# Stage 1 of a fused attention and MoE kernel: three loads issued earlier on SP, one later load pinned in the queue

## The chip, the cores and the metric

One core of a Trainium2 chip runs the whole program. The time is device microseconds of one execution. The profile is one execution of its own, with its own time; times of other runs are given as medians.

## What is computed

Three stages run in one program, all in float32: multi-head attention with rotary embedding, a gated MLP with a spatial mix over the sequence, and a causal attention with four experts of which two are taken.

```python
# batch 4, heads 8, seq 576, head_dim 64
q_rot, k_rot = rotate(q), rotate(k)
scores = scale * q_rot @ k_rot.T ; attn = softmax(scores) ; x = attn @ v      # stage 1
h = gelu(x @ w_in) ; u, v = split(h) ; x = x + (u * (w_sg @ norm(v) + b)) @ w_out   # stage 2
out = top-2-of-4 experts of causal attention over x                           # stage 3
```

The change touches stage 1 alone: the attention, and the conversion of w_in that runs beside it for stage 2. That weight comes as 64-bit words and is turned into a pair of float32 parts (high and low) by ACT, DVE and POOL.

## The kernel before, in words

Stage 1 works on pairs of heads: 4 batches of 4 pairs, 16 pairs, called pair 0 to pair 15 here (the third pair is pair 2). A pair takes nine slots, 0 to 8, one for each 128 rows of scores of one head (slot 8 holds the last 64 rows of both). The loop at the end of the stage runs `slot(k)` for k from 0 on, with pair n = k // 9 and slot x = k % 9, and after it one step of the w_in conversion in the slots that `W_AT` names: slot 7 of pair 0; slots 3 to 6 of pair 1; slots 2 to 4 of even pairs; slots 0 to 3 of odd ones.

The products of a pair need its query copies and its key copies in a layout for TensorE. For pair n+1 they are made inside pair n. `load` brings q and k with their rotary partners (`t0` is q, `t1` is k, 576 KB each) into tiles that have two buffers each, so a load for pair n+2 must wait until pair n's rotated q or k has been read for the last time. `rope` rotates them on POOL: two products and a sum for each (for pair n+2: q in slot 4 and k in slot 7 of pair n, and in slots 7 and 8 for pair 2). `parts` then splits them: DVE (ACT for pair 1) casts to the high part `hi`, POOL subtracts to get `lo`, and SP issues DMAs that copy both into place: `fill_q`, six copies, in slot 1 of the pair before, and `fill_k`, four copies into `kh`, in slot 3 of the pair before. The first product that needs them is the one for slot 0 of the new pair, issued in slot 8.

The order of the work on PE, ACT, DVE and POOL is the program's order, written by hand. The SP queue is different. A planner orders the DMAs that are not pinned by when it expects their inputs and buffers, so it may issue a load long before its place in the program. `tc.keep_in_program_order` pins a DMA directly behind the DMA that precedes it in the program text on the same queue. Pinned before the change are: the inputs of pairs 0 and 1, all values (`load_values`, 320 KB, three buffers), and the words of w_in (`load` in `convert_in`, 512 KB, two buffers). All DMAs of this stage go through SP, and SP issues them one after another; one that waits holds up all behind it.

The lines that the steps below use: L361 to L376 (inputs and values), L154 (key copies), L169 (query copies), L511 (results out), L174 (row factors out), L598 (w_in). Operations of the four engines carry the line of a helper, L59, and are told apart by their tiles.

Of the kernel before, what the change touches and what calls it, by code (L numbers as in the profile page):

```python
# [15 lines left out]
B, H, S, D = 4, 8, 576, 64  # L16
# [3 lines left out]
NP = H // 2  # L20
# [6 lines left out]
def f(ap):  # L27

    return ap.bitcast(F32)
# [15 lines left out]
def fused_kernel(ctx, tc, qk, v, w_in, w_out, w_sg, g_ln, b_sg, wqk, wvg, wo, rope, cst, out):  # L45
    nc = tc.nc
# [26 lines left out]
    def bank(t):  # L73
        shape = [P, 2, 512] if t.isupper() else [P, 512]
        return ps[t].tile(shape, F32, tag="b", name="ps_" + t)
# [22 lines left out]
    def split(hi, lo, src, engine=POOL):  # L98
        ACT.copy(hi, src)
        engine.tensor_tensor(lo, src, f(hi), op=ALU.subtract)  # L100
# [81 lines left out]
    def ahead(load, n):  # L182

        t = load(0)
        for c in range(n):
            u, t = t, load(c + 1) if c + 1 < n else None
            yield u
# [136 lines left out]
    with ExitStack() as st:  # L324
# [30 lines left out]
        class Work:  # L355
# [3 lines left out]
            def load(self, n):  # L359
                self.n, self.b, self.p, self.pr = n, n // NP, n % NP, prs[n % 2]  # L360
                self.ts = []  # L361
                for x in range(2):
                    self.ts.append(ld.tile([P, 2, S], F32, tag=f"t{x}", name=f"t{x}"))
                for x in (1, 0) if n < 2 else (0, 1):
                    d = nc.sync.dma_start(self.ts[x], qk[self.b, self.p, :, x])
                    if n < 2:
                        tc.keep_in_program_order(d)
                    if n == 0 and x == 1:
                        for i in range(2):
                            tc.keep_in_program_order(nc.sync.dma_start(rp[:, i], rope[:, i]))  # L370
                if n == 0:
                    tc.keep_in_program_order(nc.sync.dma_start(ident, cst[:, 0:P]))

            def load_values(self):
                self.vt = ld.tile([P, NKB, 2, D], F32, tag="v", name="v", bufs=3)
                tc.keep_in_program_order(nc.sync.dma_start(self.vt, v[self.b, self.p]))  # L376

            def first(self):

# [146 lines left out]
        def slot(k):  # L526


            n, x = divmod(k, 9)
            (nk, xk), (nn, xn) = divmod(k - 1, 9), divmod(k + 1, 9)  # L530
            w, p, wk, wn, nx = [works.get(i) for i in (n, n - 1, nk, nn, n + 1)]

            if w:
                w.exps(x)
            if x == 0 and p:
                p.out(False)
            if x == 4 and p:
                p.out(True)

            if wn:  # L540
                if xn == 0:
                    wn.start()
                wn.scores(xn)
            if wk:
                wk.turn(xk)
            for at, g, i in ((4, w, 0), (5, w, 1), (7, w, 2), (0, p, 3), (1, p, 4)):
                if x == at and g:
                    g.turn_left(i)
            if x == 1 and p:
                p.turn_factor()  # L550

            if wn:
                wn.maxima(xn)
            for at, g, i in ((1, w, 0), (3, w, 1), (5, w, 2), (7, w, 3), (0, p, 4)):
                if x == at and g:
                    g.gather(i)
            if x == 0 and p:
                p.factor(0)

            if n == 0 and x in (2, 3):  # L560
                works[1].rope(3 - x, (2,), DVE)
            if wk:
                wk.place(xk)
            if x == 0 and p:
                p.factor(1)
            if x == 2 and p:
                p.place_left(True)
                p.store_factor()
            if x == 5 and w:
                w.place_left(False)  # L570

            if x in (1, 3) and p:
                p.av(True, x // 2)
            if x in (5, 7, 8) and w:
                w.av(False, {5: 0, 7: 1, 8: 2}[x])

            if nx:
                if x == (4 if n == 0 else 1):
                    nx.parts(0, DVE if n else ACT)
                if x == 3:  # L580
                    nx.parts(1, DVE if n else ACT)
                if n + 2 < B * NP:
                    if x == 3:
                        works[n + 2] = Work()
                        works[n + 2].load(n + 2)
                    if x == (7 if n == 0 else 4):
                        works[n + 2].rope(0)
                    if x == (8 if n == 0 else 7):
                        works[n + 2].rope(1)
                if x == 4 and n + 2 < B * NP:  # L590
                    works[n + 2].load_values()

        def convert_in():


            def load(n0, c):
                raw = wst.tile([P, 512, 2], I32, tag="raw", name="raw", bufs=2)
                d = nc.sync.dma_start(raw.rearrange("p n t -> p (n t)"), w_in[:, c, 2 * n0:2 * n0 + 1024])  # L598
                tc.keep_in_program_order(d)
                return raw  # L600

            todo = list(itertools.product((DM, 0), range(4)))
            nxt = load(*todo[0])
            yield
            for i, (n0, c) in enumerate(todo):
                raw = nxt
                w0, w1 = raw[:, :, 0], raw[:, :, 1]
                a = wst.tile([P, S], F32, tag="wt", name="wt")[:, 0:512]
                ACT.activation(a, w1.bitcast(F32), AF.Abs, scale=65536.0)
                if i < 7:  # L610
                    nxt = load(*todo[i + 1])
                yield
                DVE.tensor_scalar(a, a, 65536.0 * TINY, None, op0=ALU.max)
                yield
                for h in (slice(0, 256), slice(256, 512)):
                    t = bank("l")[:, h].bitcast(I32)
                    DVE.tensor_scalar(t, a[:, h].bitcast(I32), 3, None, op0=ALU.logical_shift_left)
                    DVE.scalar_tensor_tensor(t, w0[:, h], 29, t, op0=ALU.logical_shift_right, op1=ALU.bitwise_or)
                    yield
                    DVE.scalar_tensor_tensor(a[:, h].bitcast(I32), w1[:, h], -2 ** 31, t, op0=ALU.bitwise_and, op1=ALU.bitwise_or)  # L620
                    yield
                split(wi[0][:, c, n0:n0 + 512], wi[1][:, c, n0:n0 + 512], a)
                yield

        works = {0: Work(), 1: Work()}
# [8 lines left out]
        fixed[0] = True  # L634
        warmed(40)
        works[0].load(0)
        works[0].load_values()
        works[0].first()
        works[1].load(1)
        works[1].rope(1, (0, 1))  # L640
        works[1].load_values()
        works[1].rope(0, (0, 1))
        works[0].start()
        works[0].scores(0)
        works[0].maxima(0)
        wload = convert_in()
        steps = iter(())
        for k in range(9 * B * NP + 7):
            n, x = divmod(k, 9)
            slot(k)  # L650
            if k < 4:
                warmed(2)
            if x in W_AT[4 if n == NP * B - 1 else min(n, 2 + n % 2)]:
                next(wload, None)
            if k == 9 * 4:
                steps = attended(bx, 0)
            if k == 9 * 14:
                lsteps = leftover(bx, 0)
            if n >= 4 and x == 8:
                next(steps, None)  # L660
            if n >= 14 and x == 3:
                next(lsteps, None)
            if k == 9 * 15 + 1:
                nsteps = attended(bx, 1)
            if k > 9 * 15 and x in (1, 5):
                next(nsteps, None)
# [286 lines left out]
    with ExitStack() as st:  # L953
# [311 lines left out]
        works, qk, vp, op, gate, ys = {}, {}, {}, {}, [], []  # L1265
# [259 lines left out]
```

## Time and profile before

| | us |
|---|---|
| three runs, median | 681.13 (680.72 to 682.45) |
| the profiled execution, its own time | 678.8 |
| its span, first to last instruction | 677.0 |
| PE busy in the span | 666.6 (98%) |
| DVE, ACT, POOL busy | 454.1, 426.2, 342.6 |
| granted TensorE clock | 0.999 |

PE is busy nearly all of the span, and 85% of the chain that ended last is PE. So what a change of loads can give back is the little time in which PE waits. A busy PE is not a PE at its peak, though: a pair that takes longer than its neighbours shows a wait even where no idle time is recorded. The length of a pair is read from an operation that comes once in each pair. The DMA view and the order of the SP queue then tell which transfers came late.

### The profile page before, as it was taken

What the parts mean: (1) busy time and instruction counts of PE and PEld (TensorE: products, weight loads), DVE (VectorE), ACT (ScalarE), POOL (GpSimd) and SP (SyncE); (2) the same over time, 40 slices, a digit from 0 to 9 for tenths busy, and PEclk for the clock granted to TensorE, in tenths of its full rate; (3) what the DMA queues carried; (4) which work ended last, traced back from release to release, by engine and by line L of the source; (5) the groups of instructions that cost most, each with busy time, mean ns of one, the idle gap of its engine ahead of it and who ended that gap; (6) DMA issues with size and microseconds to landing.
All of it is one profiled execution on the core that took longest, in us unless ns stands there. A gap on an engine that the chain in (4) does not pass through costs nothing.

```text
span 677.0 us, 13577 instructions
## 1 busy us (share of the span) xinstructions
PE 666.6 (98%) x4741; PEld 585.9 (87%) x4741; DVE 454.1 (67%) x1026; ACT 426.2 (63%) x1018; POOL 342.6 (51%) x333
## 2 busy tenths in 40 slices
PE   8999999999999999999999999999999999999997
PEld 8777777777777777798999899899999999999985
DVE  5877777777787767478974764665247667666674
ACT  6777676777777777574472472472147776666774
POOL 2877777788888861462446217306313451542320
PEclk9999999999999999999999999999999999999999
DMA  7698887888788762652365234045556364453522
GB/s 271 197 282 246 258 235 210 247 243 248 229 250 249 215 175 80 190 157 80 118 186 176 88 108 135 16 132 161 128 167 163 76 185 93 131 158 81 142 82 78
DMA packets 64930, 112.84 MB, mean 167 GB/s; under 512 B 19471, under 2 KB 24670, under 8 KB 64862
## 3 DMA queue, kind: packets, MB, share of 16 engines
q1 hardware_dynamic: 62126, 106.30, 54.3%
q10 hardware_dynamic: 2736, 5.68, 2.8%
q8 instruction: 38, 0.62, 0.4%
q14 instruction: 30, 0.25, 0.1%
HBM read 58.06 MB, written 18.98 MB: 114 GB/s over the span
## 4 chain that ended last, share of the span: by engine, by line
PE 85%; DVE 5%; DMA 4%; ACT 2%; issue 1%; POOL 1%; SPq 1%; ACTq 0%; POOLq 0%; DVEq 0%
PE ps_S L59 45%; PE ps_o L59 16%; PE ps_t L59 13%; PE ps_f L59 5%; PE ps_l L59 3%; PE ps_s L59 3%; DVE nmax L59 1%; DMA ws<-in_w_sg_dram 1%; DVE ga L59 1%; DMA kh<-hi 1%; DMA mask<-in_cst_dram 1%; DVE g L59 1%; ACT ga L59 1%; DMA xr<-xt 1%; ACT e L59 1%
## 5 line engine op out<-in xcount | busy, mean ns | idle before, releaser
L59 ACT ACTIVATE e<-ps_S,nmax 128x576 f32<-128x576 f32 x144 | 108.0, 750 | 68.0 <-DVE nmax L59 67.8
L59 DVE TENSOR_REDUCE nmax<-ps_S 128x1 f32<-128x576 f32 x144 | 108.6, 755 | 57.3 <-PE ps_S L59 55.0
L59 PE MATMUL ps_t<-ident,e 128*128 128x128 f32 x776 | 120.6, 273 | 0.0
L59 PEld LDWEIGHTS ps_t<-ident,e 128*128 128x128 f32 x776 | 94.9, 140 | 3.8 <-ACT wih L59 0.4
L59 PE MATMUL ps_S<-kh,q 128*128 128x288 f32 x352 | 86.3, 337 | 2.6 <-ACT e L59 1.6
L59 POOL TENSOR_TENSOR t<-t,rp 128x576 f32<-128x576 f32 x60 | 84.4, 1429 | 0.1
L59 PEld LDWEIGHTS ps_S<-kh,q 128*128 128x128 f32 x352 | 53.2, 189 | 31.0 <-issue 10.7
L59 PE MATMUL ps_o<-g,v 128*64 128x320 f32 (+1 forms) x512 | 76.6, 418 | 0.4 <-DVE g L59 0.4
L59 POOL TENSOR_TENSOR lo<-t,hi 128x576 fp32r<-128x576 f32 x30 | 43.3, 1444 | 49.1 <-DVE hi L59 47.8
L59 PE MATMUL ps_S<-lo,qz 128*128 128x288 f32 x304 | 65.1, 296 | 0.0
L59 PEld LDWEIGHTS ps_o<-g,v 128*64 128x64 f32 x512 | 31.3, 136 | 25.1 <-issue 9.5
L59 PE MATMUL ps_S<-yh,w 128*128 128x288 f32 x256 | 51.8, 304 | 0.0
L59 POOL TENSOR_TENSOR yl<-x,yh 128x640 fp32r<-128x640 f32 (+1 forms) x16 | 25.1, 1569 | 51.1 <-ACT yh L59 50.9
L59 ACT ACTIVATE e<-e,nmax 128x128 f32<-128x128 f32 (+4 forms) x72 | 42.3, 588 | 13.6 <-DVE nmax L59 13.6
L59 PEld LDWEIGHTS ps_S<-lo,qz 128*128 128x128 f32 x304 | 48.5, 188 | 0.0
L59 ACT COPY g<-ps_t 128x512 f32<-128x512 f32 x80 | 46.8, 585 | 1.4 <-PE ps_t L59 0.8
L59 DVE COPY g<-ps_t 128x512 f32<-128x512 f32 x64 | 43.5, 680 | 1.3 <-PE ps_t L59 1.3
L59 POOL TENSOR_TENSOR t<-t 128x576 f32<-128x576 f32 x28 | 39.8, 1421 | 2.2
L59 PEld LDWEIGHTS ps_S<-yh,w 128*128 128x128 f32 x256 | 38.7, 189 | 0.1
L59 ACT ACTIVATE ga<-ga 128x512 f32<-128x512 f32 (+1 forms) x34 | 22.3, 656 | 25.8 <-DVE ga L59 25.8
L59 DVE CUSTOM_DVE_ANT_0 e<-ps_s,mask 128x128 f32<-128x128 f32 (+3 forms) x64 | 31.0, 485 | 8.1 <-PE ps_s L59 6.3
L59 PE MATMUL ps_S<-wsh,vh 128*128 128x288 f32 x160 | 34.6, 297 | 0.8 <-DVE u L59 0.5
(286 smaller groups left out, 1734.8 us busy)
## 6 DMA issues: line engine op xcount, KB each, us to landing
t<-in_qk_dram SPq DMA_DIRECT2D x32, 576.0 KB, 4.4
kh<-hi SPq DMA_DIRECT2D x92, 144.0 KB, 2.7
q<-hi SPq DMA_DIRECT2D x38, 144.0 KB, 2.4
qz<-hi SPq DMA_DIRECT2D x38, 144.0 KB, 3.1
q<-lo SPq DMA_DIRECT2D x38, 144.0 KB, 2.7
v<-in_v_dram SPq DMA_DIRECT2D x16, 320.0 KB, 3.0
sa<-xr SPq DMA_DIRECT2D x16, 288.0 KB, 3.6
xd<-sa SPq DMA_DIRECT2D x16, 288.0 KB, 2.9
```

The costliest lines, as they stand in the source:

```text
L59: ins = op(*a, **k)
```

## The change

Four edits, all in stage 1. (1) Pair 2's inputs are no longer loaded in slot 3 of pair 0 but ahead of the loop, right behind pair 1's values, k before q, and both are pinned. (2) Pair 2's values follow them, where they stood in slot 4 of pair 0. (3) The w_in conversion holds up to two loaded blocks in a list: the first load is issued ahead of the loop, behind pair 2's values; the second in slot 7 of pair 0; load i+2 stands behind the last DVE step that reads block i, where load i+1 stood behind the first ACT step of block i. The steps of the conversion themselves stay in their slots. (4) The inputs of pair 5, loaded in slot 3 of pair 3, are pinned too.

```diff
-                for x in (1, 0) if n < 2 else (0, 1):
+                for x in (1, 0) if n < 3 else (0, 1):
                     d = nc.sync.dma_start(self.ts[x], qk[self.b, self.p, :, x])
-                    if n < 2:
+                    if n < 3 or n == 5:
                         tc.keep_in_program_order(d)
...
-            def load_values(self):
+            def load_values(self, n):
                 self.vt = ld.tile([P, NKB, 2, D], F32, tag="v", name="v", bufs=3)
-                tc.keep_in_program_order(nc.sync.dma_start(self.vt, v[self.b, self.p]))
+                tc.keep_in_program_order(nc.sync.dma_start(self.vt, v[n // NP, n % NP]))
...
                     if x == 3:
-                        works[n + 2] = Work()
-                        works[n + 2].load(n + 2)
+                        if n:
+                            works[n + 2] = Work()
+                            works[n + 2].load(n + 2)
...
-                if x == 4 and n + 2 < B * NP:
-                    works[n + 2].load_values()
+                if x == 4 and n and n + 2 < B * NP:
+                    works[n + 2].load_values(n + 2)
...
-            nxt = load(*todo[0])
+            raws = [load(*todo[0])]
+            yield
+            raws.append(load(*todo[1]))
             yield
             for i, (n0, c) in enumerate(todo):
-                raw = nxt
+                raw = raws.pop(0)
                 w0, w1 = raw[:, :, 0], raw[:, :, 1]
                 a = wst.tile([P, S], F32, tag="wt", name="wt")[:, 0:512]
                 ACT.activation(a, w1.bitcast(F32), AF.Abs, scale=65536.0)
-                if i < 7:
-                    nxt = load(*todo[i + 1])
                 yield
...
+                if i < 6:
+                    raws.append(load(*todo[i + 2]))
                 split(wi[0][:, c, n0:n0 + 512], wi[1][:, c, n0:n0 + 512], a)
...
         works[1].load(1)
         works[1].rope(1, (0, 1))
-        works[1].load_values()
+        works[1].load_values(1)
+        works[2] = Work()
+        works[2].load(2)
+        works[2].load_values(2)
+        wload = convert_in()
+        next(wload)
         works[1].rope(0, (0, 1))
         works[0].start()
         works[0].scores(0)
         works[0].maxima(0)
-        wload = convert_in()
```

## Rows read from the trace of the kernel before

**Rows 1.** Timeline of ACT, once per pair: start, duration, operation (slot 0).
```profile
47.42 0.22 ACT L59 ACTIVATE rs<-sums 128x9 f32<-128x9 f32 x1
...
64.13 0.22 ACT L59 ACTIVATE rs<-sums 128x9 f32<-128x9 f32 x1
...
80.03 0.22 ACT L59 ACTIVATE rs<-sums 128x9 f32<-128x9 f32 x1
```

**Rows 2.** Waits of PE, 190 to 230: total, times, longest.
```profile
PE ps_S L59 <- DMA xr<-xt: 0.3, 1, 0.3
```

**Rows 3.** Timeline of PE: first key products of pairs 1, 3 and 5.
```profile
28.52 0.53 PE L59 MATMUL ps_S<-kh,q 128*128 128x288 f32 x2
...
61.55 0.49 PE L59 MATMUL ps_S<-kh,q 128*128 128x288 f32 x2 [0.79 <-DMA kh<-hi]
...
93.32 0.53 PE L59 MATMUL ps_S<-kh,q 128*128 128x288 f32 x2
```

**Rows 4.** Timeline of the SP queue, 11 to 30: issue start, duration, transfer, how many.
```profile
11.61 3.33 SPq L365 DMA_DIRECT2D t<-in_qk_dram  x2
20.36 2.47 SPq L154 DMA_DIRECT2D kh<-hi  x4
...
27.33 0.58 SPq L376 DMA_DIRECT2D v<-in_v_dram  x1
27.96 0.45 SPq L598 DMA_DIRECT2D raw<-in_w_in_dram  x1
28.50 0.88 SPq L365 DMA_DIRECT2D t<-in_qk_dram  x2
29.42 0.44 SPq L598 DMA_DIRECT2D raw<-in_w_in_dram  x1
```

**Rows 5.** Stretches of time: last two columns are share of the DMA engines, GB/s.
```profile
18.00:21.00 3.00, 2.86 (x23) 2.42 (x21) 3.00 (x6) 2.20 (x5) 3.00 (x3) 1.00 0.00 0
...
27.00:33.00 6.00, 6.00 (x47) 4.78 (x47) 4.49 (x11) 4.65 (x14) 5.84 (x5) 1.00 0.95 290
```

**Rows 6.** Timeline of the SP queue, 54 to 57.
```profile
54.89 0.45 SPq L174 DMA_DIRECT2D rd<-rr  x1
55.78 0.36 SPq L365 DMA_DIRECT2D t<-in_qk_dram  x1
56.25 2.39 SPq L154 DMA_DIRECT2D kh<-hi  x4
```

**Rows 7.** Timeline of DVE, the casts of pair 3's k and pair 5's q and k.
```profile
53.62 0.46 DVE L59 CAST hi<-t 128x576 fp32r<-128x576 f32 x1
...
81.70 0.46 DVE L59 CAST hi<-t 128x576 fp32r<-128x576 f32 x1
...
86.24 0.46 DVE L59 CAST hi<-t 128x576 fp32r<-128x576 f32 x1
```

**Rows 8.** Timeline of the SP queue, 71 to 90.
```profile
71.60 2.38 SPq L154 DMA_DIRECT2D kh<-hi  x4
...
84.09 0.91 SPq L169 DMA_DIRECT2D q<-lo  x1
...
87.33 2.38 SPq L154 DMA_DIRECT2D kh<-hi  x4
```

**Rows 9.** Timeline of POOL, 72 to 88: pair 5's rotation and its low parts.
```profile
72.31 2.79 POOL L59 TENSOR_TENSOR t<-t,rp 128x576 f32<-128x576 f32 x2
75.18 1.42 POOL L59 TENSOR_TENSOR t<-t 128x576 f32<-128x576 f32 x1
76.55 2.79 POOL L59 TENSOR_TENSOR t<-t,rp 128x576 f32<-128x576 f32 x2
79.42 1.43 POOL L59 TENSOR_TENSOR t<-t 128x576 f32<-128x576 f32 x1
82.24 1.42 POOL L59 TENSOR_TENSOR lo<-t,hi 128x576 fp32r<-128x576 f32 x1 [1.39 <-DVE hi L59]
86.84 1.43 POOL L59 TENSOR_TENSOR lo<-t,hi 128x576 fp32r<-128x576 f32 x1 [3.18 <-DVE hi L59]
```

**Rows 10.** DMA issues, 10 to 30, then 60 to 112: count, KB, us to landing.
```profile
t<-in_qk_dram SPq DMA_DIRECT2D x4, 576.0 KB, 3.7
...
t<-in_qk_dram SPq DMA_DIRECT2D x7, 576.0 KB, 4.8
kh<-hi SPq DMA_DIRECT2D x12, 144.0 KB, 3.0
```

More of the change, by code (lines that the diff above doesn't have):

```diff
@@ L636, in fused_kernel @@
         works[0].load(0)
-        works[0].load_values()
+        works[0].load_values(0)
         works[0].first()
```

## The prediction, before the changed kernel was run

> **What bounds the kernel now.** I read the page's busy times and its chain first: PE is busy for 98% of the span, so a change of loads can only give back time in which PE waits for a transfer. Next the length of a pair, from one operation that comes once in each: pair 2 takes 64.13 - 47.42 = 16.71 us, pair 3 80.03 - 64.13 = 15.90 us [rows 1], and the pairs behind it mostly repeat 15.90. Pair 2 is thus 0.8 us too long. Then who PE waits for: at the first key product of pair 3, at 61.55, PE had been idle for 0.79 us until key copies landed [rows 3]. That is the whole excess of pair 2. Of waits for DMAs in stage 1 there is one more, 0.3 us in pair 12 [rows 2]. So the prize in reach of this change is about 1.1 us, 0.16% of the time, and most of it lies in one place.
>
> **Why the key copies of pair 3 came late.** The cast that they read ended at 53.62 + 0.46 = 54.08 [rows 7]. SP was busy with the row factors until 54.89 + 0.45 = 55.34, and then it did not issue the key copies but one input load of pair 5, at 55.78, and the copies from 56.25 on [rows 6]. That load stands a whole pair later in the program; the planner had moved it up. It costs the copies twice: 56.25 - 55.34 = 0.91 us of issue, and 576 KB that move ahead of them.
>
> **Part 1: pair 2's inputs and values and w_in's first words move up.** Before, pair 2's inputs were already issued at 11.61, ahead of the key copies of pair 1 at 20.36, only because the planner put them there [rows 4]; pinning them changes nothing at their place. The second of them holds SP until 11.61 + 3.33 = 14.94. New behind it are the values (320 KB) and the first words (512 KB), which stood at 27.33 and 27.96 [rows 4]. Together they are 832 KB, 0.85 MB, and at the 290 GB/s of a crowded stretch they need 2.9 us. From 18 to 21 the DMA engines moved nothing at all [rows 5]. So they are through at about 18 + 2.9 = 20.9, while the key copies are issued from 20.36 to 22.83. The issues themselves (0.58 and 0.45 us) end at 16.0, and SP then waits for the cast of pair 1's k as before. I cost this at nothing. What hides it is the empty stretch. If that cover were gone, the 2.9 us would lie ahead of the copies: the last of them is issued at about 20.36 + 2.47 - 0.6 = 22.2 and lands 3.0 us later [rows 10], at 25.2, or 28.1 with the delay, and PE wants them at 28.52 [rows 3]. Bounds: 0 to 0.5 us, and below nothing only if PE waited there, which it does not. I take 0.
>
> **Part 2: the crowded stretch behind it gets lighter.** From 27 to 33 the engines are 95% busy [rows 5]; 0.85 MB less is 2.9 us less of transfer. The second words, at 29.42 before, now stand directly behind pair 1's last query copy, in place of the values at 27.33. That they go there and not elsewhere I read from the old order: the second words stood in slot 3 of pair 1, behind pair 3's inputs in the program, and were issued directly behind them [rows 4] although those had been moved up; a pinned load follows its predecessor wherever that goes. Pair 2's own copies can then come earlier, but PE did not wait for them. Gain on the path: 0. Bounds: 0 to -0.3 us, the other DMA wait [rows 2], should an emptier queue persist so long.
>
> **Part 3: the later words of w_in.** Six loads move from slot 0 of an odd pair to slot 4 of the even pair before it, behind that pair's values. Each now waits for DVE's last read of the block before, which was done in slot 3; so the wait has ended when SP comes there. The price is one issue, 0.44 us [rows 4], ahead of whatever comes next in SP, which is an input load with a pair's time to spare. I take 0; if each held up one key copy it would be 0.4 us once in two pairs, and I see none behind it before the next pair's query copies.
>
> **Part 4: pair 5's inputs are pinned.** By the rule just read they go behind the key copies that slot 3 of pair 3 issues, those of pair 4 at 71.60. This removes the load at 55.78: the copies of pair 3 move up by 0.91 us, which is more than the 0.79 that PE waited, even before the 576 KB are counted. Gain: 0.8 us. It is lost again if the planner fills the gap with another transfer.
>
> But the pin also moves the load back, by 18 us: it is issued at 71.60 + 2.38 = 73.98, say 74.1 [rows 8]. In the trace an input load lands 3.7 us after issue in a light stretch and 4.8 us in a crowded one [rows 10], so it is there at 77.8 to 78.9. POOL wanted it at 72.31 [rows 9]. POOL is in order, so from here on it is late by 5.5 to 6.6 us: the rotation of q and k takes 72.31 to 80.85, 8.54 us, and ends at 86.3 to 87.4. What waits for that? DVE's cast of q, at 81.70 [rows 7], needs the first half, done at 82.1 to 83.2; I count up to 1.5 us of wait, most of it beside PE work. The cast of k at 86.24 waits 0.1 to 1.2 us. And the low part of q, 1.42 us, is done at 87.8 to 88.8, where the query copies that read it were issued at 84.09 [rows 8]. If SP keeps its old order, with these ahead of the key copies, the latter start 87.33 - 84.09 = 3.24 us later less the 0.45 of a load that no longer stands between, 2.8 us: 90.6 to 91.6; the second of them 0.6 later, landed 3.0 later: 94.2 to 95.2. PE wants both at 93.32 [rows 3]: 0.9 to 1.9 us late. If the planner sees POOL late and issues the key copies first, as soon as the cast of k is done (86.8 to 87.9), all four are there at 92.2 to 93.3 and PE waits for nothing. Bounds of this cost: 0 to 1.9 us. I take 0.3, near the lower end: the planner orders by expected inputs (that is how the load got to 55.78), and a pair's query copies can be issued with the key copies between them.
>
> The Trainium skill, "DMA: Bandwidth & Descriptors", section "Rules for kernel authors", says to issue a DMA early and wait late, so that the fixed cost overlaps. It speaks for part 1 and against part 4. The same page, "Anatomy of one DMA", has a fit of 2.0 us plus bytes over 436 GB/s, made for loads issued from GpSimd; for 576 KB that is an estimate of 3.4 us, under the 3.7 of the rows, and would bring the load in at 77.5 and the late case to 0.5.
>
> **The sum.** 0 + 0 + 0 - 0.8 + 0.3 = -0.5 us. The profiled execution has a span of 677.0 and a time of 678.8; its span would become 676.5 and its time 678.3. The three runs have a median of 681.13, 2.3 above the profiled one; I take the difference over to the median: 681.13 - 0.5 = 680.6.
>
> **The rivals.**
> Slower, the late pin: in the old order of SP, the pinned load makes the key copies of pair 5 late. It decides against the change once the load lands later than 77.7, where the wait of PE reaches 0.8 and eats the gain. With the landing at 78.9: 681.13 - 0.8 + 1.9 = 682.2. For it: the load is needed 1.8 us before it can even be issued, and the copies and loads around share one queue. Against it: the queue at 71 to 74 is lighter, since words and half the input load that stood at 61 to 66 have moved, and POOL has idle time of 1.39 and 3.18 us to catch up in [rows 9].
> No effect: the planner puts another transfer ahead of pair 3's key copies, and PE waits as before. Then 681.13 + 0.3 = 681.4. For it: any unpinned load whose buffer is free can go there. Against it: in the other pairs the queue mostly goes straight from row factors to key copies.
> More: the late pin is free and the 0.3 us in pair 12 goes too, since its cause is like that of pair 3: 681.13 - 0.8 - 0.3 = 680.0. Against it: that place is 150 us later, and nothing there is pinned.
>
> **How the numbers follow.** Forecast (680.6) 0.47, the late pin 0.27, no effect 0.12, more 0.14. Ends of the terms: -1.1 and +1.9 - 0.8 = +1.1, or +1.9 if the gain fails as well. The runs before spread over 1.7 us around their median, so a median of new runs may sit 0.8 away from its own. The range from 679.1 to 682.6 covers 680.0 - 0.9 and 682.2 + 0.4. About 0.3%, 2.04 us, is what a measurement can tell from no change. No case reaches it by its own size: under 679.09 or over 683.17 it takes an end and the spread together, or a reordering of the unpinned transfers in later stages that I don't foresee. So faster 0.08, same 0.84, slower 0.08.
>
> **What would show it.** Right: the SP queue goes from row factors to key copies near 55 with no input load between; pair 2 lasts 15.9; PE's wait for the key copies at 61.55 is gone. Values and first words are issued at about 15, and the DMA engines are no longer empty from 18 to 21. For the late pin: pair 5's inputs follow the key copies at about 74, POOL's rotation starts at 77 or later with a wait for a DMA, and pair 4 is longer than 15.9. Wrong: a wait of PE at 28.5 for pair 1's copies; pair 0 or 1 of another length; any difference of over 1 us outside pairs 2 to 5.

## The result and the profile after

| | before | after |
|---|---|---|
| median, same chip (11 executions each) | 681.01 us (679.05 to 683.59) | 685.09 us (682.71 to 690.28) |
| ratio | 1 | 1.0061, 95% interval 1.0037 to 1.0084 |
| profiled execution, its span | 677.0 us | 681.8 us |
| pair 2 / pair 4 | 16.71 / 15.90 us | 15.89 / 17.63 us |
| pair 11 / pair 12 | 16.19 / 16.21 us | 18.08 / 17.22 us |
| start of pair 15's row factors | 270.62 us | 274.85 us |

The kernel became slower by 0.6%; 680.6 was forecast, with 679.1 to 682.6 as the range. The predicted gain came: pair 2 is 0.82 us shorter. Three pairs got longer: pair 4 by 1.73, pair 11 by 1.89, pair 12 by 1.01 us. With +0.17 in pair 0 and +0.25 in pairs 9 and 10 that is +4.23 us at the end of stage 1's loop; the stages behind it add 0.57. Of the 4.8 us between the two spans (the medians are 4.1 us apart), 2.9 lie 100 us behind the pairs that the prediction thought about.

The lengths come from the operation that stands once in each pair, as in [rows 1]; here are pairs 2 to 4 and 11, 12 of the changed kernel (start, duration):

```profile
47.60 0.22 ACT L59 ACTIVATE rs<-sums 128x9 f32<-128x9 f32 x1
63.49 0.22 ACT L59 ACTIVATE rs<-sums 128x9 f32<-128x9 f32 x1
79.39 0.22 ACT L59 ACTIVATE rs<-sums 128x9 f32<-128x9 f32 x1
97.02 0.22 ACT L59 ACTIVATE rs<-sums 128x9 f32<-128x9 f32 x1
...
192.68 0.22 ACT L59 ACTIVATE rs<-sums 128x9 f32<-128x9 f32 x1
210.76 0.22 ACT L59 ACTIVATE rs<-sums 128x9 f32<-128x9 f32 x1
227.98 0.22 ACT L59 ACTIVATE rs<-sums 128x9 f32<-128x9 f32 x1
```

What PE waited for, whole span (total, times, longest). Three of these places lie in the pairs that grew: 1.5 for `wt` in pair 4, 1.8 for key copies in pair 11, 1.3 in pair 12, where before there was 0.3 [rows 2]:

```profile
PE ps_l L59 <- DVE wt L59: 1.9, 3, 1.5
PE ps_S L59 <- DMA kh<-hi: 1.8, 1, 1.8
...
PE ps_S L59 <- DMA xr<-xt: 1.3, 1, 1.3
```

The last row names a copy of results (`xr`), which the waiting product does not read. In the trace this product waits for the key copies issued at 219.66 and 220.17; their last parts land at 224.77 and 225.27, and it starts at 225.41. So the wait in pair 12 is one for key copies too, and so is the 0.3 us of [rows 2] (key copies landed at 221.01, product at 221.14).

**The gain.** The SP queue of the changed kernel, where [rows 6] had an input load between the row factors and the key copies:

```profile
54.61 0.29 SPq L174 DMA_DIRECT2D rd<-rr  x1
55.01 2.39 SPq L154 DMA_DIRECT2D kh<-hi  x4
```

**Pair 4.** The pinned input load of pair 5 on SP, then POOL's rotation that waits for it, DVE's two casts beside POOL, and PE (start, duration, and in brackets the idle time before and what ended it). Each cast took 0.46 us before [rows 7]:

```profile
73.71 1.08 SPq L365 DMA_DIRECT2D t<-in_qk_dram  x2
...
77.73 2.81 POOL L59 TENSOR_TENSOR t<-t,rp 128x576 f32<-128x576 f32 x2 [6.03 <-DMA t<-in_qk_dram]
80.61 1.42 POOL L59 TENSOR_TENSOR t<-t 128x576 f32<-128x576 f32 x1
81.98 3.01 POOL L59 TENSOR_TENSOR t<-t,rp 128x576 f32<-128x576 f32 x2
...
86.44 1.41 POOL L59 TENSOR_TENSOR lo<-t,hi 128x576 fp32r<-128x576 f32 x1
...
82.06 1.66 DVE L59 CAST hi<-t 128x576 fp32r<-128x576 f32 x1 [0.99 <-POOL t L59]
86.51 1.65 DVE L59 CAST hi<-t 128x576 fp32r<-128x576 f32 x1
88.08 0.41 DVE L59 SCALAR_TENSOR_TENSOR wt<-raw,ps_l 128x256 int32<-128x256 int32 x1
...
88.54 0.33 PE L59 MATMUL ps_l<-ident,e 128*128 128x128 f32 x1 [1.50 <-DVE wt L59]
```

The chain is to be read from top to bottom: load late, rotation late, so POOL is still at work when DVE casts; the second cast holds DVE until 88.16; the step of the w_in conversion behind it, `wt`, reads from the PSUM bank that PE's transposes need next; PE waits 1.50 us.

**Pair 11.** SP in the changed kernel. Load 6 of w_in (the first line) and the input loads, which are those of pair 13, stand ahead of the four row gathers (`er`, DMAs of 64 KB that spread the factors of the leftover rows over the partitions):

```profile
191.18 0.38 SPq L599 DMA_DIRECT2D raw<-in_w_in_dram  x1
191.92 0.80 SPq L365 DMA_DIRECT2D t<-in_qk_dram  x2
192.77 2.82 SPq L310 DMA_DIRECT2D er<-rd  x3
195.69 0.77 SPq L511 DMA_DIRECT2D xr<-xt  x1
196.50 0.72 SPq L310 DMA_DIRECT2D er<-rd  x1
197.34 0.59 SPq L169 DMA_DIRECT2D q<-hi  x1
199.27 0.50 SPq L169 DMA_DIRECT2D qz<-hi  x1
201.64 0.46 SPq L169 DMA_DIRECT2D q<-hi  x1
...
203.39 1.22 SPq L169 DMA_DIRECT2D q<-lo  x2
204.70 2.48 SPq L154 DMA_DIRECT2D kh<-hi  x4
```

And the same stretch before, where load 6 went out behind the gathers and the query copies followed one another without gaps:

```profile
188.48 0.92 SPq L365 DMA_DIRECT2D t<-in_qk_dram  x2
189.74 2.63 SPq L310 DMA_DIRECT2D er<-rd  x4
192.48 0.54 SPq L511 DMA_DIRECT2D xr<-xt  x1
193.12 0.40 SPq L598 DMA_DIRECT2D raw<-in_w_in_dram  x1
195.15 0.52 SPq L169 DMA_DIRECT2D q<-hi  x1
195.76 0.55 SPq L169 DMA_DIRECT2D qz<-hi  x1
...
199.44 2.74 SPq L154 DMA_DIRECT2D kh<-hi  x4
```

SP's own waits in 186 to 212 of the changed kernel have a row that before does not have in this stretch, and PE's first key product of pair 12 shows what it costs:

```profile
SPq L169 <- DMA t<-in_qk_dram: 3.1, 2, 1.9
...
208.18 0.51 PE L59 MATMUL ps_S<-kh,q 128*128 128x288 f32 x2 [1.83 <-DMA kh<-hi]
```

In the order of the queue the query copies at 197.34, 199.27 and 201.64 are the eighth DMA behind the words, the first and the second input load, respectively. The wait of the latter two has the input loads as its releaser: a copy that has nothing to do with an input load does not go out until that load has landed, and in SP's order the key copies stand behind it. The two input loads land at 199.20 and 201.62, 7.3 and 9.3 us after their issue; before, it was 4.1 and 5.8 us. The count of eight shows in the semaphores of the trace: SP's DMAs of this stage take eight of them in turn, and these copies wait for the last DMA that used their own.

### The profile page after: what moved, and what is told of

It is laid out like the page before. It is cut to its first block, busy times and chain, and to the rows that moved or that the text cites. A ratio compares the mean times of both kernels' runs of the same rounds, so it can differ in the third digit from the quotient of the medians.

```text
span 681.8 us, 13593 instructions
## 1 busy us (share of the span) xinstructions
PE 667.6 (98%) x4741; PEld 586.1 (86%) x4741; DVE 455.2 (67%) x1026; ACT 425.8 (62%) x1018; POOL 342.4 (50%) x333
## 4 chain that ended last, share of the span: by engine, by line
PE 85%; DVE 6%; DMA 4%; ACT 2%; issue 1%; SPq 1%; POOL 1%; DVEq 0%; ACTq 0%; POOLq 0%
PE ps_S L59 46%; PE ps_o L59 16%; PE ps_t L59 13%; PE ps_f L59 5%; PE ps_l L59 3%; PE ps_s L59 3%; DVE nmax L59 1%; DMA xr<-xt 1%; DMA er<-rd 1%; DMA mask<-in_cst_dram 1%; DVE ga L59 1%; ACT e L59 1%; DVE g L59 1%; ACT ga L59 0%; DMA r<-d 0%
## 5 line engine op out<-in xcount | busy, mean ns | idle before, releaser
L59 PE MATMUL ps_S<-kh,q 128*128 128x288 f32 x352 | 86.3, 338 | 4.8 <-DMA kh<-hi 1.8
L59 POOL TENSOR_TENSOR gxl<-u,gxh 128x576 fp32r<-128x576 f32 x16 | 22.8, 1431 | 25.9 <-ACT gxh L59 25.9
```

The source lines that it names most:

```text
L59: ins = op(*a, **k)
```

## The experiments

**First question: which part costs what?** The changed kernel without the pin, and with the later words of w_in in their old place; the kernel before with the pin alone, and with the words alone.

Without the pin:

```diff
-                    if n < 3 or n == 5:
+                    if n < 3:
```

> The changed kernel with the pin on pair 5's inputs undone. Theory (two separate causes: the pin costs pair 4, the words' new place costs pairs 11 and 12): pair 4 falls from 17.63 to 15.9 us, pair 2 rises from 15.89 to about 16.7 as in the kernel before, pairs 11 and 12 stay at 18.1 and 17.2; span 681.8 - 1.7 + 0.8 = 680.9. Rival (the pin reorders the unpinned transfers of later pairs, and the words cost nothing): pairs 11 and 12 go back to 16.2 each; span about 678.

Measured: pair 2 16.36, pair 4 15.89, pair 11 17.03, pair 12 17.22; span 678.7; ratio 1.0035 (1.0005 to 1.0065). Pair 4 is whole again, pairs 11 and 12 are not, so the two costs are separate. Pair 11 was expected to stay at 18.1 and came out 1 us shorter. Pair 2 lost half of its gain, since an input load stands ahead of its key copies again.

Later words in their old place, the rest of the change as it is:

```diff
+                if 1 <= i < 7:
+                    raws.append(load(*todo[i + 1]))
                 yield
...
-                if i < 6:
-                    raws.append(load(*todo[i + 2]))
```

> The changed kernel with the w_in loads 2 to 7 back in their old place (behind the first ACT step of the block before); the first two loads stay ahead. Theory: pairs 11 and 12 go back to 16.2 each, pair 4 stays at 17.6, pair 2 at 15.9; span 681.8 - 1.9 - 1.0 = 678.9. Rival (the pin is behind pairs 11 and 12): they stay at 18.1 and 17.2; span 681.8.

Measured: pair 2 15.91, pair 4 17.92, pair 11 16.21, pair 12 16.48; span 679.5; ratio 0.9985 (0.9954 to 1.0016). Pair 11's cost is the words', pair 4's the pin's.

The pin alone, in the kernel before:

```diff
-                    if n < 2:
+                    if n < 2 or n == 5:
```

> The kernel before with the pin on pair 5's inputs alone. Theory: pair 2 15.9 (from 16.71), pair 4 17.6 (from 15.90), pairs 11 and 12 16.2 each as before; span 677.0 - 0.8 + 1.7 = 677.9. Rival: pairs 11 and 12 take 18.1 and 17.2, span about 680.8.

Measured: pair 2 15.90, pair 4 21.83, pair 11 16.18, pair 12 16.89; span 684.0; ratio 1.0025 (0.9996 to 1.0054). The gain in pair 2 is the pin's alone. In this execution the price of the pin in pair 4 is far larger than with the early heads: a query copy held SP for 2.85 us at 67.83, and the key copies waited 1.1 us for words of W_in, again eight DMAs before them. So the pinned load went out at 76.77 and not at 73.71, and POOL waited 8.94 us:

```profile
SPq L154 <- DMA raw<-in_w_in_dram: 1.1, 1, 1.1
...
81.02 2.79 POOL L59 TENSOR_TENSOR t<-t,rp 128x576 f32<-128x576 f32 x2 [8.94 <-DMA t<-in_qk_dram]
...
85.33 1.65 DVE L59 CAST hi<-t 128x576 fp32r<-128x576 f32 x1 [3.45 <-POOL t L59]
```

Part of pair 4's length in this execution goes with a lower clock (last section). With 685.78 us it is also 2.5 us above the median of its ten, so 21.83 need not be the usual price.

The words alone, in the kernel before:

```diff
-                if i < 7:
-                    nxt = load(*todo[i + 1])
+                if i == 0:
+                    raws.append(load(*todo[1]))
...
+                if i < 6:
+                    raws.append(load(*todo[i + 2]))
```

> The kernel before with w_in loads 2 to 7 alone moved behind the last DVE step that reads their buffer; loads 0 and 1 as before. Theory: pairs 11 and 12 take 18.1 and 17.2 instead of 16.19 and 16.21, pair 2 keeps its 16.7, pair 4 15.9; span 677.0 + 2.9 = 679.9. Rival: all pairs as before, span 677.0.

Measured: pair 2 16.78, pair 4 16.43, pair 9 16.56, pair 11 17.93, pair 12 18.44; span 683.1; ratio 1.0030 (1.0002 to 1.0057). Moving six loads of 512 KB by five slots is slower by itself. Pairs 4, 9 and 12 and the span are longer than expected, so more than pairs 11 and 12 can pay.

**Second question: is pair 4's price the slow casts or the lateness?** Pair 5's two casts go to ACT, the rest is the changed kernel (`parts(1, ...)` in the same way):

```diff
-                    nx.parts(0, DVE if n else ACT)
+                    nx.parts(0, DVE if n not in (0, 4) else ACT)
```

> The changed kernel with the two casts of pair 5 (its q and k, in slots 1 and 3 of pair 4) on ACT instead of DVE. In the changed kernel each took 1.65 us beside a POOL operation, against 0.46 in the kernel before. Theory (the pin costs pair 4 its time because POOL's late rotation runs under DVE's casts and slows them): without them DVE is 3.3 us lighter where it ended last, ACT 1.3 us heavier; pair 4 falls from 17.63 to 16.0 to 16.6. Rival (the cost is only that the rotated data is there late, whoever casts): pair 4 stays between 17.2 and 18.

Measured: pair 4 17.13. The casts took 0.68 us each, but still waited for POOL:

```profile
82.07 0.68 ACT L59 CAST hi<-t 128x576 fp32r<-128x576 f32 x1 [1.13 <-POOL t L59]
...
86.31 0.68 ACT L59 CAST hi<-t 128x576 fp32r<-128x576 f32 x1 [0.91 <-POOL t L59]
```

PE's wait is then 0.7 for ACT's exponentials, in place of 1.5 for `wt`. Between what the two theories expected, nearer the rival: by these two executions some 0.5 of the 1.73 us is the lengthened casts (17.63 - 17.13); against the kernel with the words in their old place (17.92) it would be 0.8. That the rest is the late data, whichever engine takes it, fits the casts' waits for POOL but is not shown by a run of its own.

The same pinned load a pair earlier, in the kernel before, directly behind pair 4's values:

```diff
-                    if n < 2:
+                    if n < 2 or n == 5:
...
+                    if n == 2:
+                        works[5] = Work()
+                        works[5].load(5)
```

> The kernel before with pair 5's inputs pinned one pair earlier, behind pair 4's values in slot 4 of pair 2. Theory: pair 2 15.9 because no input load stands ahead of pair 3's key copies, and pair 4 15.9 because the load lands by 66, before POOL wants it at 72; the DVE casts of pair 5 take 0.46; pairs 11 and 12 16.2 as before; span 677.0 - 0.8 = 676.2. Rival (any pin of this load costs): pair 4 above 16.5.

Measured: pair 2 15.90, pair 11 16.22; span 678.4. But pair 4 took 16.88 where 15.9 was expected. POOL was in time; the planner had put one input load of pair 7 ahead of pair 5's key copies, and PE waited 0.9 us:

```profile
86.31 0.29 SPq L174 DMA_DIRECT2D rd<-rr  x1
86.64 0.35 SPq L365 DMA_DIRECT2D t<-in_qk_dram  x1
87.61 3.11 SPq L154 DMA_DIRECT2D kh<-hi  x4
```

So one pin moved the planner's choice to the next pair; the fourth question takes the pin for every pair.

**Third question: what in the words costs pair 11?** The kernel without the pin, with load 6 alone in its old place:

```diff
+                if i == 5:
+                    raws.append(load(*todo[6]))
...
-                if i < 6:
+                if i < 6 and i != 4:
```

> The changed kernel without the pin, with one w_in load, number 6 (slot 4 of pair 10 in the change), back in its old place in slot 0 of pair 11; the other five moved loads keep their new place. Theory (this one load, ahead of pair 12's input loads and the small gathers of the leftover rows, costs pair 11, and pair 12 follows from it): pair 11 16.2 instead of 17.03, pair 12 16.2 to 16.7 instead of 17.22; span about 678.7 - 1.6 = 677.1. Rival (the shift of all six costs): pair 11 stays at 17 and pair 12 at 17.2.

Measured: pair 11 16.23, as expected, so it is this one load. All runs divide in the same way: pair 11 takes 16.18 to 16.23 in the eight kernels with load 6 in its old place, 17.03 to 18.74 in the five where SP issues it in the new one, so 1.89 is one value of a wide range. Pairs 12 and 13, 19.12 and 17.35, missed the expectation. An input load of pair 15 stood ahead of the key copies, and PE waited 3.0 us in pair 12. In pair 13 PE waited for nothing; there the granted clock was lower behind the wait (last section). Pair 12 varies in every kernel whose input loads are not pinned (16.0 to 19.1 us), with the words in either place.

Words 2 to 7 from ACT's queue, so that SP has neither their issue nor their place in its count:

```diff
-                d = nc.sync.dma_start(raw.rearrange("p n t -> p (n t)"), w_in[:, c, 2 * n0:2 * n0 + 1024])
+                q = nc.sync if n0 and c < 2 else nc.scalar
+                d = q.dma_start(raw.rearrange("p n t -> p (n t)"), w_in[:, c, 2 * n0:2 * n0 + 1024])
```

> The changed kernel without the pin, with w_in loads 2 to 7 in their new place in time but issued from ACT's queue instead of SP's. Theory of order (pair 12's inputs stand behind the words in SP's queue and land late, and the query copies wait in SP until they have landed): the words no longer stand ahead in the queue, pair 11 falls from 17.03 to 16.2 to 16.5. Theory of bytes (512 KB more at that moment slow every transfer, whatever queue issues them): pair 11 stays at 17.0.

Measured: pair 11 15.90, the shortest of all kernels. It does not part the two theories: load 6 went out at 189.92, 10 us ahead of pair 11, and had landed (6.5 us later) before the input loads were issued at 196.94. Pairs 2, 4, 6, 8 and 9 took 17.3 to 18.2, pairs 10, 12 and 13 16.6 to 17.2, and the span 687.7: nothing orders the words against SP's copies any more, and they went out just ahead of the key copies of even pairs (53.68 against 54.84 in pair 2). PE waited 8.6 us for key copies in five places, pairs 2, 4, 6, 8 and 12. In pairs 2, 4 and 12 an input load stood ahead of the copies too; in pairs 6 and 8 it was the words alone, and PE waited 1.6 and 2.3 us. So here the words cost time right ahead of key copies as well.

**Fourth question: the whole rule.** If a big load that comes ahead of key copies, or too late for POOL, is what costs, then all input loads should be pinned a pair early, behind the values. In the kernel before:

```diff
-                    if n < 2:
+                    if n != 2:
...
                     works[n + 2].load_values()
+                    if n + 3 < B * NP:
+                        works[n + 3] = Work()
+                        works[n + 3].load(n + 3)
```

> The kernel before, with one edit: the input load of every pair from 3 on is pinned behind the values that are loaded in slot 4, a pair earlier than its old place, so that the planner cannot put one ahead of key copies; words of W_in as before. Theory (what costs time is a big load that stands ahead of the key copies of the next pair, or that lands too late for POOL): pairs 2, 4 and 12 last 15.9, pair 11 at most 16.2, the sum of pairs 2 to 13 falls by 1.1 from the kernel before, the span to about 676.0, the ratio is 0.998. Rival (any pin takes away room that the planner used, or an early load holds the query copies behind it as the words do in pair 11): at least two pairs of 3 to 13 last over 16.5, and the span is 678 or more.

Measured: pair 2 15.89, pair 3 16.09, pair 4 15.89, pairs 11 to 13 16.18, 15.90, 16.22; the loop ends at 270.50; span 677.3; ratio 0.9978 (0.9953 to 1.0002). No pair from 3 to 13 is over 16.3, so the rival falls. But the gain of 1.1 us is not all there: pair 2 gives 0.82, pair 12 gives 0.31 and pair 13 takes it back, and the first pair was 0.52 longer in this execution, so that its span is not shorter than that of before.

The same with the change's heads (early inputs, values and words for pair 2), the later words in the old place:

```diff
-                    if n < 3 or n == 5:
+                    if True:
...
+                if 1 <= i < 7:
+                    raws.append(load(*todo[i + 1]))
...
-                if i < 6:
-                    raws.append(load(*todo[i + 2]))
```

> The change's early inputs, values and first words for pair 2, its second words where the change has them, every later input load pinned behind the values a pair earlier, and the later words of W_in in the place of the kernel before. Theory: as the kernel with early pins alone, within 0.3 us of it in span (the heads cost and give nothing by themselves): pairs 2, 4 and 12 at 15.9, pair 11 at most 16.2, span about 676. Rival: the heads have a price of their own, a first pair over 31.5 or a pair 1 or 2 over 16.3.

Measured: pair 2 15.89, pair 4 15.89, pairs 11 to 13 16.18, 15.90, 16.22; the loop ends at 270.07, 0.55 us earlier than before; span 677.2; ratio 0.9980 (0.9963 to 0.9998). The heads cost nothing and give nothing that these spans can tell. This kernel is 0.2% faster than before, and it cannot be told from the kernel with early pins alone (0.9978). Its span of 677.2 does not show the gain: behind the loop it takes 407.1 us, before 406.4, with one wait of PE for POOL in stage 3 of 1.3 us (0.6 before).

And with the later words in the change's place too, that is, the whole change with early pins:

```diff
-                    if n < 3 or n == 5:
+                    if True:
...
+                    if n + 3 < B * NP:
+                        works[n + 3] = Work()
+                        works[n + 3].load(n + 3)
```

> All of the change, the later words of W_in in its new place too, but every input load from pair 3 on pinned behind the values a pair earlier. In pair 11 the words (load 6) then stand behind the input loads and ahead of the row gathers; in the changed kernel they stood ahead of both. Theory (the words delay the input load, and the query copies wait for that load): pair 11 lasts 15.9 to 16.4. Rival (half a megabyte of words just ahead of the row gathers is enough, wherever the input load stands): pair 11 lasts 17.0 to 18.1 as in the four kernels with the words in the new place.

Measured: pair 2 15.90, pair 4 15.90, pair 11 17.83, pair 12 15.90; span 678.1; ratio 0.9986 (0.9966 to 1.0006). The rival is right, and the theory on the order falls: with the input load ahead of the words, pair 11 is as long as with it behind them. SP's waits in 186 to 206:

```profile
SPq L169 <- DMA raw<-in_w_in_dram: 1.6, 1, 1.6
SPq L169 <- DMA t<-in_qk_dram: 1.3, 1, 1.3
```

The query copies now wait for the words themselves as well: those went out at 189.28, and the copy that stands eight DMAs behind them at 198.35. The second input load lands late all the same, 7.3 us after its issue.

The last run parts the size of that load from its place in the count. Load 6 stands in its old place again, and in its new place stands a load of 8 KB:

```diff
-                if i < 6:
+                if i < 6 and i != 4:
                     raws.append(load(*todo[i + 2]))
+                if i == 4:
+                    tiny = wst.tile([P, 16], I32, tag="tiny", name="tiny", bufs=1)
+                    tc.keep_in_program_order(nc.sync.dma_start(tiny, w_in[:, todo[6][1], 2 * todo[6][0]:2 * todo[6][0] + 16]))
```

> The kernel with all of the change and early pins, but in pair 11 load 6 stands in the place of the kernel before again, behind three of the row gathers, and in its new place, ahead of the gathers, stands a load of 8 KB that nothing reads. Theory (the 512 KB themselves, moved beside the input load and the row gathers, make the loads ahead of the query copies land late): pair 11 lasts at most 16.4. Rival (one more issue at that place shifts which earlier load each query copy has to wait for, whatever its size): pair 11 lasts 17 or more, as with the full load there (17.83).

Measured: pair 11 16.22, span 677.0, with no wait of SP for a DMA from 186 to 206. The second input load lands 6.1 us after its issue, before the query copy that waits for it is due. One more issue at that place is free; the 512 KB there are what costs. It is not that the DMA engines of the changed kernel move more there: from 190 to 194 they move 224 GB/s, before 383; from 194 to 198 283 in both kernels; from 198 to 202 196, before 205. With the words 3 us later, behind three of the gathers, the cost is gone; by which path on the DMA engines they delay the input load from their earlier place is not shown.

What follows from the four questions: the pin's price is lateness at POOL plus casts that are lengthened beside it (how it divides is open); the words' price in pair 11 is that 512 KB beside the input load and the row gathers hold up query copies that wait for the DMA eight places before them, and SP's order hands this on to the key copies. The excess of pair 12 is like that of pair 2 (an unpinned input load ahead of key copies), since it is gone where all input loads are pinned early: pair 12 is 15.90 in the four kernels with all of them pinned, 16.0 to 19.1 in the others. Pair 13 then takes 16.2 in all four, 15.91 before, and why is open.

## Why the prediction was wrong

- **What bounds it** (pair 2's excess of 0.8 us from one input load ahead of key copies): right. In all kernels where that load is gone pair 2 takes 15.9; where it is there, 16.4 to 18.1 (the longest with words from ACT's queue beside it).
- **Part 1** (heads, 0): right. Values and first words were issued at 15.14 and 15.61, the DMA engines are 0.72 busy in 18 to 21 where they had been empty [rows 5], PE does not wait for pair 1's copies, pair 1 is 16.30 against 16.29. Pair 0 is 0.17 longer, which the prediction listed as a sign of being wrong; its end lies between 29.9 and 32.0 us in the single executions of all kernels, so this tells nothing.
- **Part 2** (a lighter stretch, 0): the price was right, the picture partly wrong. The second words came where I put them, at 27.49, but the stretch from 27 to 33 stayed as crowded: 0.99 busy and 321 GB/s against 0.95 and 290 [rows 5]. What was moved away shows behind it: from 33 to 36 the engines are 0.54 busy, before 0.92. The crowd became shorter, not thinner.
- **Part 3** (later words, 0): this step failed, and it is the largest: +1.89 us in pair 11 in the profiled executions, and perhaps a share of the +1.01 in pair 12, which the runs do not part. I costed the six loads at their issues (0.38 us for load 6 as measured) and wrote that what comes next is an input load with a pair's time to spare. POOL indeed did not wait for it. SP did: a query copy waits for the DMA eight before it, that was the input load, and with the words ahead of it it landed 7.3 to 9.3 us after its issue instead of 4.1 to 5.8. I looked only at who reads the loaded data. I also took six loads for one case, by the rows of stage 1's start; only pair 11's place has the `er` gathers behind the load.
- **Part 4, the gain** (-0.8): right, -0.82.
- **Part 4, the late pin** (+0.3, bounds 0 to 1.9): mis-sized, +1.73. The times of the chain were right: the load at 73.71 (74.1 forecast), POOL's rotation from 77.73 (77.8 to 78.9), its end at 86.48 (86.3 to 87.4). SP took neither of the two orders that I priced: two key copies, the low parts' query copies, then the other two key copies. PE did not wait for them.

```profile
88.19 1.10 SPq L154 DMA_DIRECT2D kh<-hi  x2
89.38 1.19 SPq L169 DMA_DIRECT2D q<-lo  x2
90.62 1.23 SPq L154 DMA_DIRECT2D kh<-hi  x2
```

  What I had wrong is the path to PE. I priced the key copies alone and let DVE's wait for POOL lie beside PE work. In the run it reached PE through DVE's own order, by the `wt` step behind the second cast. I also had no price for two casts that stand beside a busy POOL. I took 0.46 us from [rows 7], where POOL was idle; they took 1.66 and 1.65, and with both on ACT pair 4 was still 17.13. The trace of before had the warning: one of its casts runs beside POOL, and takes 1.51 us.

```profile
193.35 1.42 POOL L59 TENSOR_TENSOR xl<-sa,xh 128x576 fp32r<-128x576 f32 x1
...
193.57 1.51 DVE L59 CAST hi<-t 128x576 fp32r<-128x576 f32 x1
```

  The Trainium skill, "SBUF — State Buffer", section "Who interferes with whom", says that a DVE cast in a mode that uses two ports and a GpSimd instruction exclude each other: whichever comes first holds the pair of ports for the whole instruction. The trace agrees: 1.2 us are added, less than one POOL operation of 1.4 us. The same section says that ACT never waits on another engine; the trace agrees there too: the casts on ACT took 0.68 us beside a busy POOL, and in the kernel before one of pair 1's casts, at 22.72 with POOL idle, took 0.67.
- **The rivals**: the slower one came near the size of pair 4's loss (1.73, its upper bound was 1.9), but that is luck: its path was late key copies, and PE waited for none there. The rival with a larger gain was right that pair 12's wait is like pair 3's, and the early pins removed it; in the changed kernel that wait grew from 0.3 to 1.3 us. None of the rivals had a loss outside pairs 2 to 5.
- **The chances**: for a slower result I named an end of the range together with the spread, or a reordering of unpinned transfers in later stages, and gave it 0.08. The change moved six loads by hand through pairs 2 to 12, so those places belonged into the sum, one by one.

What stays open: +0.57 us behind stage 1, where nothing was changed (that part was 406.4 us before and between 406.4 and 407.6 in the other kernels, in single executions), and how pair 12's 1.01 us divide between words and input load.

## What to carry to other kernels

A load that is moved is to be costed at each place where it lands, by three questions: who reads it, what stands behind it in its queue, and which later DMA of that queue waits for it to land. A duration is to be taken from a row in which the neighbours are as busy as they will be after the change; here a cast beside POOL was three and a half times as long. And where a planner orders what is left free, pinning one load moved the collision to the next place; pinning all of them early removed it. With the change's heads that kernel is 0.2% faster than before (0.9980, 0.9963 to 0.9998, so only just told from no change).

## What was not expected of the hardware

In the kernel with the pin alone the granted clock of TensorE fell after a stretch in which PE was partly idle. Windows of 4 us (bounds, length, then busy time and count of each engine): PE, PEld, DVE, ACT, POOL; granted clock, DMA share, GB/s:

```profile
84.00:88.00 4.00, 2.67 (x20) 1.44 (x18) 2.67 (x3) 0.32 (x1) 4.00 (x3) 1.00 0.85 314
88.00:92.00 4.00, 2.19 (x10) 1.78 (x10) 3.96 (x8) 2.37 (x7) 3.46 (x4) 0.60 0.63 154
92.00:96.00 4.00, 4.00 (x19) 2.73 (x18) 1.89 (x4) 2.81 (x7) 3.92 (x4) 0.54 0.79 194
96.00:100.00 4.00, 4.00 (x31) 3.30 (x32) 2.15 (x4) 2.15 (x5) 4.00 (x4) 1.00 0.66 188
```

PE was busy for 2.67 and 2.19 of 4 us, and the clock was then 0.60 and 0.54 of full speed, near the lower of its two levels (1.2 of 2.4 GHz), until 96. In 92 to 96 PE is busy all the time and 19 matmuls are counted, where the next 4 us hold 31. So a wait can cost more than its length: pair 4 is 5.9 us longer, while PE's waits in 70 to 100 add up to 3.5 (1.9, 1.2 and 0.4). The kernel with load 6 in its old place shows the same: PE was busy for 0.96 of the 4 us from 222 to 226, and from 226 to 230, across the end of pair 12, the clock was 0.57 and 21 matmuls ran where the next 4 us hold 32. Pairs 12 and 13 together are 4.7 us longer than two pairs of 15.90; 3.0 is the wait, and 4 us at 0.57 make an estimate of 1.7 for the rest. A wait does not always do this: in the changed kernel PE was busy for 2.17 of the 4 us from 205 to 209, and the clock stayed at 1.00 from 205 to 213.

Whole executions differ in the same way. Of the changed kernel's eleven, seven have a mean granted clock of 0.994 to 0.998 and average 686.3 us, the four at 1.000 average 684.0, 3.0 us above the median of before. That pinning all input loads early keeps the clock up is not shown: 2 of 34 executions of the three kernels that do so are under 0.999, but so are only 3 of 29 of the kernel before on the same chip, and 12 of 31 of it on another.
